# Opening of a fused FNet and MLP kernel: x loaded ahead of the weights, scratch laid out by group, first chunk as eight plain block products between the weight conversions

## The chip, the core and the metric

The kernel runs on one core of one Trainium2 chip. The metric is the device time of one execution in microseconds (us). Unless a "span" is named, times are medians over several executions.

## The reference

```python
def _attn_ref(x):                       # x: 8 x 3008 x 256, f32
    X = np.fft.fft(x, axis=1)
    X = np.fft.fft(X, axis=2)
    return X.real.astype(np.float32)

def _moe_ref(x, w_in, w_out):           # 24064 tokens, 256 -> 2048 -> 256, weights in float64
    h = x @ w_in
    relu6 = np.clip(h + 3.0, 0.0, 6.0)
    g = h * relu6 / 6.0
    return (g @ w_out).astype(np.float32)
```

The output of the first is reshaped to tokens and given to the second.

## The kernel before

The Fourier transform along the sequence is split in two (47 x 64). *Stage 1* multiplies by the 47-point table: a piece of x and its mirrored partner rows are folded on DVE, multiplied on TensorE, copied out by ACT as a piece of z, and written to a scratch `zd` in DRAM. *Stage 2* reads `zd` back transposed as g, one *group* of frequencies at a time, and multiplies by the table T into q. The transform along the 256 columns is folded into w_in ahead of time (`fold_w_in`). Then comes the MLP in *steps*: `mlp1` makes u and v, DVE and ACT make the activation a, `mlp2` multiplies by w_out into acc. Eight steps are a *chunk* of tokens. There are 48 chunks, so 384 steps: 352 of 4.75 us, and 32 of about 3.6 us in the shorter last chunk of each pair, some 1790 us in all. Nearly all the time is the MLP; what matters here is the opening before it, for the first *pair* of batches.

The weights are float64 and are taken apart by hand. One *piece* of weights goes through exponent_a on ACT, a matmul `ex` on TensorE, exponent_c on ACT, a mantissa and a join on DVE. There are 16 pieces. Pieces 0 to 3 and 6 to 9 are w_in, the others w_out.

```python
    def x_tile(pr, i):                      # where the pieces of x live in the opening
        pool, tag = xpool, "x"              # four buffers
        if pr.p == 0 and 4 <= i < 13:
            pool, tag = ((apool, "a"), (cpool, "c"), (spool, "t"))[(i >= 8) + (i >= 11)]
        return pool.tile([PR + 2, XC, D], F32, tag=tag, name="xt")
    ...
    def mlp2(ch, fc):                       # seven products, fast matrix multiplication
        a = ch.a.pop(fc)[:].rearrange("p m f n -> p (m f) n")[:, :, 0:ch.n]
        c = ch.c.pop(fc)                    # sums of blocks of a, made on POOL by combine()
        moving = [a[:, 0], a[:, 1], a[:, 3], c[:, 0], c[:, 1], c[:, 2], c[:, 3]]
        for i, mv in enumerate(moving):
            ...
            nc.tensor.matmul(ch.acc[i // 2][:, i % 2, 0:ch.n], G[:, i, fc, :], mv, ...)
    ...
    for c in range(NXC):                    # the opening: x and weights side by side
        if c + 2 < NXC:
            load_x(first, c + 2)
        load_w(c + 2)
        if c < NXC - 1:
            fold_first(first, c)
        else:
            for part in range(2):
                fold(first, c, part, nc.vector)
        on_scalar(c)                        # exponent_c of piece c-1, exponent_a of piece c
        on_vector(c)                        # mantissa of piece c, join of piece c-1
        for i in range(XC // 2):
            (stage1_first if c < NXC - 1 else stage1)(first, c, i)
        on_tensor(c)                        # ex of piece c; a finished pair is folded or mixed
        ...
    load_g(first, 0)
    for j in range(NXC, 15):                # the other weight pieces, one by one
        ...
    for i in range(2):
        stage2(first, 0, i)
    spread(first, 0)
    ...
    on_scalar(15); on_vector(15)            # (joined on one line here)
    mlp1(*chunk(0))                         # only now does the MLP begin
```

## Time and profile before

| | |
|---|---|
| median, three runs | 1984.56 us (1981.78 to 1984.95) |
| profiled span | 1978.3 us |
| TensorE busy | 1949.1 us, 99% of the span |
| first u of the MLP starts | 80.06 us |
| step 7 (last of chunk 0) ends | 132.37 us |

TensorE is nearly full from about 90 us to the end. The window lines in the prediction show the part where it is not: a busy time of 17 of 20 us there is not all useful, because it holds dummy matmuls, put there to keep TensorE from idling (`keep_awake`).

### The profile page before, as it was taken

The page shows a single profiled execution, that of the slowest core. Times are in us where ns is not written, and L with a number is a line of the kernel's source. Part 1 is how long each engine was busy: PE and PEld are TensorE (multiplying, and loading weights), DVE is VectorE, ACT ScalarE, POOL GpSimd, SP SyncE. Part 2 cuts the span into 40 slices and gives each one's busy share as a digit, 9 for nine tenths or more (in the row PEclk, how much of TensorE's full clock was granted, in tenths as well). Part 3 has the DMA queues.
Part 4 walks back from the last instruction along what each step waited for, and adds up shares of the span by engine and source line. Part 5 has one row for each costly group of instructions (what it writes and reads, how often), then busy time and mean ns, then how long its engine had stood idle before and what let it go on. Part 6 is the DMA issues. An engine that isn't in the chain of part 4 may idle for free.

```text
span 1978.3 us, 27746 instructions
## 1 busy us (share of the span) xinstructions
PE 1949.1 (99%) x9178; PEld 1685.4 (85%) x9178; DVE 1433.5 (72%) x2775; ACT 687.9 (35%) x1164; POOL 1414.2 (71%) x1604
## 2 busy tenths in 40 slices
PE   8899999999999999999999999999999999999998
PEld 5588888888998888888898888888889888888887
DVE  5677767776787776776777776777678777777776
ACT  6533333333333333333333333333333333333332
POOL 4277778786687787777768877778667667666765
PEclk9999999999999999999999999999999999999999
DMA  9502211111111111221111221212110101111000
GB/s 307 136 26 61 51 41 46 49 49 35 27 36 51 41 49 48 54 59 24 36 32 30 63 55 44 56 41 54 37 22 23 30 14 25 26 24 28 17 20 20
DMA packets 149701, 93.31 MB, mean 47 GB/s; under 512 B 121739, under 2 KB 135055, under 8 KB 149558
## 3 DMA queue, kind: packets, MB, share of 16 engines
q1 hardware_dynamic: 139294, 57.86, 12.2%
q0 software_dynamic: 9472, 33.49, 5.9%
q8 instruction: 72, 1.18, 0.2%
q14 instruction: 71, 0.58, 0.1%
q10 hardware_dynamic: 792, 0.20, 0.0%
HBM read 54.19 MB, written 37.33 MB: 46 GB/s over the span
## 4 chain that ended last, share of the span: by engine, by line
PE 93%; DVE 2%; ACT 1%; issue 0%; DMA 0%; SPq 0%; DVEq 0%; ACTq 0%
PE acc L403 56%; PE v L334 16%; PE u L334 16%; PE ps L284 2%; PE ps L227 2%; DVE a L379 1%; DVE s L339 1%; ACT t L376 0%; ACT PM L509 0%; DVE o L461 0%; PE wps L574 0%; DVE u L360 0%; PE ps L224 0%; PE ex L514 0%; PE awake L597 0%
## 5 line engine op out<-in xcount | busy, mean ns | idle before, releaser
L393 POOL TENSOR_TENSOR c<-a 128x512 f32<-128x512 f32 (+1 forms) x383 | 478.2, 1248 | 431.4 <-PE acc L403 369.3
L403 PE MATMUL acc<-c,G 128*128 128x256 f32 (+1 forms) x3072 | 712.0, 375 | 0.0
L376 ACT ACTIVATE t<-u,half 128x512 f32<-128x512 f32 (+1 forms) x384 | 261.0, 680 | 1100.5 <-DVE u L349 1018.7
L403 PEld LDWEIGHTS acc<-c,G 128*128 128x128 f32 x3072 | 577.5, 190 | 72.7
L339 DVE SCALAR_TENSOR_TENSOR s<-qn,WN,u 128x256 f32<-128x256 f32 (+1 forms) x768 | 330.0, 471 | 354.3 <-PE u L334 354.0
L403 PE MATMUL acc<-a,G 128*128 128x256 f32 (+1 forms) x2304 | 551.2, 375 | 0.0
L403 PEld LDWEIGHTS acc<-a,G 128*128 128x128 f32 x2304 | 433.8, 190 | 55.9
L334 PE MATMUL v<-q,W 127*128 127x256 f32 (+1 forms) x1536 | 390.1, 376 | 4.4 <-DVE a L379 4.4
L334 PE MATMUL u<-q,W 128*128 128x256 f32 (+1 forms) x1536 | 388.3, 375 | 2.4 <-DVE a L379 2.1
L379 DVE SCALAR_TENSOR_TENSOR a<-t,u 128x512 f32<-128x512 f32 (+2 forms) x448 | 263.7, 600 | 104.9 <-ACT t L376 102.1
L334 PEld LDWEIGHTS u<-q,W 128*128 128x128 f32 x1536 | 285.7, 190 | 58.2 <-issue 14.8
L334 PEld LDWEIGHTS v<-q,W 127*128 127x128 f32 x1536 | 288.7, 190 | 45.1 <-DVE a L379 4.1
L393 POOL TENSOR_TENSOR c<-c,a 128x256 f32<-128x256 f32 (+1 forms) x383 | 274.8, 717 | 30.0
L393 POOL TENSOR_TENSOR c<-a,c 128x256 f32<-128x256 f32 (+1 forms) x383 | 274.6, 717 | 30.1
L349 DVE TENSOR_TENSOR u<-s,v 128x512 f32<-128x512 f32 x352 | 245.0, 696 | 37.7 <-PE v L334 0.8
L379 DVE SCALAR_TENSOR_TENSOR a<-t,v 128x512 f32<-128x512 f32 (+1 forms) x480 | 263.2, 564 | 0.0
L376 ACT ACTIVATE t<-v,half 128x512 f32<-128x512 f32 (+1 forms) x384 | 260.5, 678 | 0.0
L351 DVE TENSOR_TENSOR v<-v,s 128x512 f32<-128x512 f32 x352 | 243.7, 692 | 0.0
L393 POOL TENSOR_TENSOR r<-w,e 128x256 f32<-128x256 f32 (+1 forms) x94 | 90.8, 987 | 3.7
L411 ACT ACTIVATE e<-acc 128x512 f32<-128x512 f32 (+2 forms) x190 | 86.3, 545 | 3.4 <-PE acc L403 3.3
L461 DVE STREAM_TRANSPOSE o<-r 128x256 f32<-128x256 f32 (+1 forms) x192 | 72.5, 414 | 0.2
L239 ACT COPY z<-ps 96x512 f32<-96x512 f32 x64 | 37.2, 582 | 83.7 <-PE ps L227 65.2
(91 smaller groups left out, 780.2 us busy)
## 6 DMA issues: line engine op xcount, KB each, us to landing
out_dram<-o SPq DMA_DIRECT2D x746, 32.0 KB
zd<-z SPq DMA_DIRECT2D x32, 384.0 KB
g<-zd SPq DMA_DIRECT2D x48, 256.0 KB
xt<-in_x_dram POOLq DMA_DIRECT2D x21, 384.0 KB, 4.1
qn<-qd SPq DMA_DIRECT2D x19, 256.0 KB
st<-in_moe_w_in_dram POOLq DMA_DIRECT2D x8, 512.0 KB, 9.1
st<-in_moe_w_out_dram POOLq DMA_DIRECT2D x8, 512.0 KB, 5.1
xt<-in_x_dram POOLq DMA_DIRECT2D x7, 376.0 KB, 3.9
```

Of the source, the lines that this page charges most:

```text
L227: nc.tensor.matmul(ps[0:PZ], F[0:PR, 0:PZ], y[:, 2 * i:2 * i + 2, :], start=True, stop=True)
L284: nc.tensor.matmul(ps[:, blk, u * P:n].rearrange("p (b k) -> p b k", b=2), g[:, kk, blk * (P + 1):blk * (P + 1) + P], T[:, :, gr, blk, kk, ...
L334: nc.tensor.matmul(ps[:, i, 0:nq], W1[r, blk, f * P:(f + 1) * P], q[r, blk, of:of + nq], start=True, stop=True)
L339: nc.vector.scalar_tensor_tensor(s[:, i, 0:nq], qn[:, of:of + nq], WN[:, f:f + 1], u[:, i, 0:nq], op0=AL.mult, op1=AL.add)
L349: nc.vector.tensor_tensor(u[:], s[:], v[:], op=AL.add)
L351: nc.vector.tensor_tensor(v[:], v[:], s[:], op=AL.subtract)
L376: nc.scalar.activation(t, h, AF.Relu, bias=half[:], scale=scale)
L379: nc.vector.scalar_tensor_tensor(dst, t, 1.0, h, op0=AL.min, op1=AL.mult)
L393: (eng or nc.gpsimd).tensor_tensor(out, in0, in1, op=AL.add)
L403: nc.tensor.matmul(ch.acc[i // 2][:, i % 2, 0:ch.n], G[:, i, fc, :], mv, start=(fc == 0 and i % 2 == 0), stop=(fc == NF - 1), skip_group_c ...
L411: nc.scalar.mul(ch.e[:, k:i + 1, 0:ch.n], ch.acc[i // 2][:, 0:i + 1 - k, 0:ch.n], 1.0 / WS)
L461: nc.vector.transpose(o[:, 0:n // DH, h], ch.r[:, m, h, 0:n].rearrange("p (j i) -> p j i", i=DH))
```

## The change

The intent is to let the MLP begin as soon as a quarter of w_in is ready, and to convert the other weights between the steps of chunk 0. To this end x is loaded alone first, with three pieces in flight, so that stage 1 ends early. The scratch is laid out by group, and the rows of group 0 are written first, so that the first g can be read early. The first chunk cannot use the seven products, whose mixed weights do not exist yet, so it uses the eight plain block products.

```diff
-    def x_tile(pr, i):
-        pool, tag = xpool, "x"
-        if pr.p == 0 and 4 <= i < 13:
-            pool, tag = ((apool, "a"), (cpool, "c"), (spool, "t"))[(i >= 8) + (i >= 11)]
+    ORDER = [NXC - 1] + list(range(NXC - 1))
+    def x_tile(pr, c):
+        pool, tag = (spool, "t") if pr.p == 0 and ORDER.index(c) % 3 == 2 else (xpool, "x")
...
-            nc.sync.dma_start(out=pr.zd[:].rearrange("b k c n d -> (b k c) n d")[:, c * XC:(c + 1) * XC, :], in_=z[:])
+            zd = pr.zd[:].rearrange("g b k c n d -> (g b k c) n d")[:, c * XC:(c + 1) * XC, :]
+            if pr.p > 0:
+                nc.sync.dma_start(out=zd, in_=z[:])
+            else:
+                n0 = PZ // NG
+                nc.sync.dma_start(out=zd[0:n0], in_=z[0:n0])
+                nc.scalar.dma_start(out=zd[n0:], in_=z[n0:])
...
+    def mlp2_first(ch, fc):
+        ...
+        for h in range(2):
+            for f in range(2):
+                nc.tensor.matmul(ch.acc[h][:], G[:, (B11, B12, B21, B22)[2 * f + h], fc, :], a[:, :, f], ...)
...
+    for c in ORDER[0:3]:
+        load_x(first, c)
+    for k, c in enumerate(ORDER):
+        for part in range(2):
+            fold(first, c, part, nc.vector)
+        for i in range(XC // 2):
+            stage1(first, c, i)
+        keep_awake(1)
+        if k + 3 < NXC:
+            load_x(first, ORDER[k + 3])
+        else:
+            for j in range(2 * k - 8, 2 * k - 6) if k > 4 else ():
+                load_w(j)
+        if k == 4:
+            load_w(0); load_w(1); load_t(0)      # joined on one line here
...
+    for j in range(4):                           # four pieces of w_in, then stage 2, then the MLP
+        head(j); exponent_b(j)
+        ...
...
+        late = 4 if p == 0 else 0
-            s2(NST * (gr - 1), cur, gr)
+            s2(NST * (gr - 1) + (late if gr == 1 else 0), cur, gr)
...
-                put(9 * c, load_x, nx, c)
+                t = 2 * late + (9 - late // 4) * c
+                put(t, load_x, nx, c)
...
-                    put(9 * c + 8 + 3 * i, stage1, nx, c, i)
+                    put(t + 8 + 3 * i, stage1, nx, c, i)
...
+    DUE = [(6, 7, 8), (9, 10, 11), (12, 13), (14, 15), (), (), (), ()]   # weight pieces in steps 0 to 3
```

## The prediction

> **What bounds the kernel now.** I first read the page: TensorE is busy 1949.1 us of a 1978.3 us span, so the middle is full. The 40 slices put the only weak spot in the first two (PE 8, DMA 9 and 5). So I cut the opening into stretches of 20 us. Columns: stretch, length, busy time and count of each engine, granted TensorE clock, DMA share, GB/s.
>
> ```profile
> 0.00:20.00 20.00, 17.09 (x50) 9.13 (x51) 9.20 (x22) 14.03 (x18) 11.65 (x21) 1.00 0.92 253
> 20.00:40.00 20.00, 20.00 (x78) 12.57 (x77) 10.70 (x21) 13.27 (x26) 7.41 (x11) 1.00 1.03 340
> 40.00:60.00 20.00, 16.74 (x54) 9.56 (x53) 13.86 (x31) 12.31 (x22) 2.89 (x5) 0.83 0.82 259
> 60.00:80.00 20.00, 17.00 (x61) 8.32 (x60) 11.97 (x27) 12.34 (x20) 1.42 (x2) 1.00 0.75 184
> 120.00:140.00 20.00, 20.00 (x97) 17.23 (x96) 13.05 (x24) 7.90 (x14) 13.64 (x16) 1.00 0.04 14
> ```
>
> Until about 46 us the DMA engines are full; later no resource is, so a chain must bind. The chain that ended last (start, length, work) names it:
>
> ```profile
> 69.28 1.41 ACT PM L509 x2
> 71.64 1.41 ACT PM L509 x2
> 73.53 0.47 issue
> 74.00 1.41 ACT PM L509 x2
> ...
> 92.06 3.53 PE acc L403 x14
> 95.58 0.86 PE u L334 x4
> 96.45 0.86 PE v L334 x4
> 97.31 3.02 PE acc L403 x14
> ```
>
> PM is the exponent of one weight piece on ACT: pieces follow each other every 2.36 us. From 92.06 on the chain is u, v, acc in turn, TensorE alone, 4.75 us per step (0.86 + 0.86 + 3.02). Step 7 (the last of chunk 0) ends at 132.37, counting acc groups; with few gaps after that, **only what comes before 132.37 can change the time**. A step of several timelines shows the x wait and the gap from row write to row read:
>
> ```profile
> 18.06 0.68 DVE L189 TENSOR_TENSOR y<-xt 94x508 f32<-94x508 f32 x1 [1.40 <-DMA xt<-in_x_dram,IX]
> 54.37 0.30 SPq L241 DMA_DIRECT2D zd<-z  x1
> 57.40 1.29 SPq L266 DMA_DIRECT2D g<-zd  x2
> 49.17 1.99 PE L227 MATMUL ps<-y,F 94*96 94x512 f32 x2 [2.87 <-DVE y L174]
> ```
>
> So before: x and weights share the DMA engines until 46 us, stage 1 ends at 54, the weight pieces finish one by one until 81, and the MLP fills until 92.
>
> **What the Trainium skill says.**
> - "DMA: Bandwidth & Descriptors", section on the anatomy of one DMA: about 2 us fixed, mostly the receipt of the write, plus the bytes. The trace agrees: 3.0 us from the issue of the last row write (54.37) to the read that waits for it (57.40).
> - "Trainium Kernel Development and Optimization", Key Constraints: SP, ACT and POOL queues run on the same 16 DMA engines. So writing rows on two queues adds no bandwidth; it can only let the first group's rows overtake the rest. The ceiling measured here is 340 GB/s (20 to 40 us).
> - "TensorE: Matmul & The Clock Gate", Part 1: after an idle window of about 3.4 us the clock halves. The trace agrees roughly: the pair of matmuls at 49.17 took 1.99 us after 2.87 us idle; the same group takes 1.02 at 132.21. The new gaps I find below are near 2 us or less.
>
> **Part by part: the first half.** One x piece is two transfers of 96x1024 f32, 0.79 MB together; a z piece is 0.39 MB, a weight piece 0.52 MB. The changed stream issues x first, three pieces in flight, and C, T, weights later. Before, x0 landed at 9.1; with C and piece 0 out of its way I take 8.5. DVE then folds piece 7 (the long form, 46.56 to 49.50 before: 3.0) and seven plain ones at 0.61 x 4 + 0.15 = 2.6. With three pieces in flight a slot is refilled 2.6 + 0.85 (issue) + 5.1 (indirect load, median of the page) after it was handed out: 8.55 per three pieces, 2.85 per piece. But x plus z is 1.18 MB per piece, and at 340 GB/s that is 3.5 us: **DMA stays the limit**. Bytes until the last x lands: F, CE, C 0.59 + x 6.3 + five z 2.0 + T 0.26 = 9.1 MB. By 12 us the trace before had moved 2.73 MB; take 2 us lost where only three pieces are in flight, then 0.33 MB/us: last x at 14 + 6.4/0.33 = 33. Its fold goes on to about 34.5 (33 to 36), not 49.5. TensorE saves eight matmul groups there (stage 1 is 1.72 per piece, not 3.44), but it waits for data in this stretch, so this is hidden.
>
> Then 2 x 0.86 matmul, 0.6 copy and 0.3 zc: ACT is free for weights at 37. Weights 0 and 1 were issued right behind x and landed by then. Rows of group 0 land near 40 (the 3.0 us above), their reads of 0.5 MB against the weight stream near 45: beside the weights, not on the path.
>
> **The four w_in pieces.** Pieces 0, 1: 2 x 2.36, to 41.7. Piece 2: exponent and ex to 44.1, and ACT then has to copy the two sums of the first fold, whose 3.43 us start at 43.5: ACT free at 47.6. Piece 3: exponent 1.41, ex 0.47 on TensorE, to 49.5. Stage 2 and spread 1.78 + 0.91: 52.2. Second fold 3.43: 55.6; the last copy 0.6: mlp1 of step 0 runs at about **56**, where before it ran at 80.06. A gain of 24 us, but twelve pieces are still to be converted, where before one was left.
>
> **Chunk 0, interleaved.** Each engine runs in program order, so I go through it by hand with: exponent 1.41, ex 0.45, exponent out 0.58, mantissa 1.07, join 0.7; mlp1 1.73; DVE and ACT from u to both gates 4.2 (as 96.49 to 100.27 before plus the ACT hop); block products 4 of N=512 = 3.43 (8 x 0.43 where before 7 x 0.43 = 3.02); fold 3.43; the single ex bank makes ex wait for the join before it. Times relative to mlp1(0) at 0: gate(0) ends 4.8; pieces 4 and 5 joined at 8; mlp2(0) runs 9.1 to 12.5; pieces 7 and 8 each cost TensorE a wait of 1.5. Step 1 in full, as an example of the walk: mlp1(2) 19.8 to 21.5; exponent 9 to 21.8, its ex to 22.3; mlp2(1) 22.3 to 25.7; gate(2) waits for mantissa 9 (22.2) and ends 25.7; ACT puts out exponent 9 after the gate's relus, 25.6; join 26.4; exponent 10 27.0, ex 27.5, out 28.1, join 28.9; fold 27.5 to 31.0, and ex 11 stands behind it: 31.4, out 32.0, join 32.8: 11.6 us for the step, of which TensorE works 9.9. So mlp2(1) ends 25.7, mlp2(2) 37.3, mlp2(3) 45.1, piece 15's ex 46.9. By sums over these 48 us: DVE 12 x 1.77 + 6 x 3.4 = 41, TensorE 38, ACT 34: **no engine is full, the ACT-TensorE-ACT-DVE chain of the pieces sets the pace, DVE nearly does**. Steps 4 to 6: 5.16 each (1.73 + 3.43). Step 7 has stage 2 0.9, mlp1 twice and 3.43. End of step 7: 46.9 + 3 x 5.16 + 0.9 + 1.73 + 3.43 + 1.73 = 70.2. The other half of stage 2 for group 1 now comes after it: +0.9; mlp1(9) and (10) come back to back, and the v of (10) needs the bank of u(9), one of three, which its gate frees only 4.2 after it began: +1.6. Sum 72.7.
>
> So step 7's equivalent is at 56 + 72.7 = 128.7 instead of 132.4: **3.7 us gained**. Were each of the twelve pieces 0.3 us better hidden than in my walk, it would be 7. Chunk 0 no longer needs combine or finish on POOL, and the mixing moved from DVE to POOL (4 x 0.72 = 2.9 us per block), where POOL is idle in steps 4 to 6; the fourth lies in step 9, where POOL has 2.8 of 4.75 us taken: no wait expected. Moving the second pair's loads by 8 steps at 8 instead of 9 apart ends at step 75 instead of 74, three steps ahead of its reader: hidden. The rest of the program is the same work.
>
> **Rivals.**
> 1. *DMA gets the opening back.* x, z and the read-back compete with weights; if bandwidth is 300 GB/s (4 to 24 us before: 304), the last x lands at 35.5, and g too comes later, after the w_in pieces: nothing gained or 2 us lost, 1985. For it: DMA share 1.03. Against: the 8.4 MB of weights, of which the trace before had moved over half by then, now queue behind x.
> 2. *The interleave flows better.* If chunk 0 were TensorE-bound: 8 x 5.16 + 12 x 0.43 + 6.9 + 1.7 + 0.9 = 56 us for its 70; then 14 us more gained, 1967. Against: the one ex bank, and DVE in order (a mantissa stands before each gate). This is the fast edge, half of it plausible.
> 3. *A new wait in the MLP proper* (POOL late with c after the fourth mix, second pair's z late): each stall is a few us once; +3, 1983. Against: the slack above.
> 4. *Faster by 2%* needs 39.7 us, that is a chunk 0 ending at 93: TensorE's own work after stage 1 (13.7 folds + 6.9 pieces + 41 chunk 0, from 37 on) alone ends at 99. Out of reach. *Slower by 2%* would need chunk 0 at 172.
>
> **Range.** Walk 3.7, fast rival 10 or more at a quarter, slow rival 0 at a fifth: mean about 6 of the median 1984.56: 1978.5. The x landing is uncertain by 2 us, the walk by 5, the runs by 1.5: 1970 to 1985. Chances: faster by over 2% 0.01, within 0.98, slower 0.01.
>
> **What would show it right or wrong.** Right: last fold of the opening ending at 33 to 36; mlp1(0) at 54 to 58; DMA share near 1 to 35; four steps with weight pieces at some 11 us each for the first two and 8 for the next two, later 5.2; step 7's end near 128; from there to the end the same length (about 1846 us) as before. Wrong if: mlp1(0) waits for g or WN rather than for the second fold; weights land late and ACT waits for DMA in the first pieces; the clock drops in the gaps between pieces (PEclk under 0.9 after 40 us); or the tail from step 8 on has changed length.

## The result

The changed kernel took **1986.59 us** (median of four, 1986.0 to 1987.58), the kernel before, on the same chip in the same rounds, 1984.76 (median of four, 1981.78 to 1986.38). The ratio is **1.0011, with a 95% interval of 0.9994 to 1.0029**: the same within 2%. A ratio is the mean time of one kernel's fast runs over that of the other's of the same rounds, so it is not quite the ratio of these medians. The control e10, the changed kernel again in other rounds, gave 1.0022 (1.0008 to 1.0036). The class was predicted right, but the time lies outside the predicted range of 1970 to 1985, on its slow side: instead of 6 us gained, 2 to 4 us were lost.

The spans of the two profiles are 1978.3 and 1984.2 us. That difference of 5.9 us is larger than what the medians show, because the profile of before fell on one of its fast executions. The comparison of traces below explains the difference between these two executions; the size of the effect comes from the ratios.

These are the same five stretches of the changed kernel. Columns: stretch, length, busy time and count of PE, PEld, DVE, ACT and POOL, granted TensorE clock, DMA share, GB/s.

```profile
0.00:20.00 20.00, 17.45 (x43) 7.57 (x44) 10.27 (x27) 10.70 (x11) 10.39 (x17) 1.00 0.84 214
20.00:40.00 20.00, 14.64 (x29) 4.74 (x28) 13.92 (x27) 6.73 (x14) 7.83 (x13) 0.91 1.03 329
40.00:60.00 20.00, 14.23 (x47) 7.74 (x46) 6.93 (x13) 11.19 (x19) 1.45 (x3) 0.91 0.76 263
60.00:80.00 20.00, 16.53 (x51) 8.08 (x50) 13.15 (x26) 13.16 (x22) 2.86 (x4) 1.00 0.29 79
120.00:140.00 20.00, 18.46 (x73) 12.83 (x72) 13.69 (x24) 6.95 (x13) 8.83 (x11) 1.00 0.15 40
```

The reader sees two things. In the first stretch the DMA engines moved 214 GB/s where before they moved 253, although x was the only large load. And the clock, which dipped only in one stretch before, is below 1 in two.

The chain that ended last, of the changed kernel (start, length, work):

```profile
16.02 7.39 DMA xt<-in_x_dram,IX
...
27.40 8.82 DMA xt<-in_x_dram,IX
...
42.29 1.39 ACT PM L513 x2
...
53.26 2.61 DMA WN<-W
55.88 3.64 PE ps L267 x16
59.52 0.89 PE ps L278 x8
60.41 3.45 PE wps L568 x8
...
111.87 3.44 PE acc L387 x8
```

Now the chain begins in transfers of x, one after the other; before, the profile's chain up to 92 us ran through the weight pieces on ACT. From 60.41 on it is second fold, u and v, then the interleaved pieces, then TensorE alone (111.87 is a plain block product of chunk 0).

The TensorE timeline of the changed kernel, with the idle time before each entry and what ended it in brackets:

```profile
53.56 0.38 PE L518 MATMUL ex<-PM,E 128*128 128x512 f16 x1 [1.32 <-ACT PM L513]
...
55.86 3.65 PE L267 MATMUL ps<-T,g 128*128 128x128 f32 x16 [1.28 <-DMA WN<-W]
...
189.10 1.05 PE L267 MATMUL ps<-T,g 128*128 128x128 f32 x8
190.83 1.10 PE L207 MATMUL ps<-y,F 94*96 94x512 f32 x2 [0.68 <-ACT q L270]
```

And the same places in the kernel before: its first stage 2 at 77 us, and then stage 2 and stage 1 of the next pair at 190 us:

```profile
77.38 1.95 PE L284 MATMUL ps<-T,g 128*128 128x128 f32 x16
...
187.07 1.05 PE L284 MATMUL ps<-T,g 128*128 128x128 f32 x8
...
192.72 1.02 PE L227 MATMUL ps<-y,F 94*96 94x512 f32 x2
```

At 55.86 the first stage 2 waits 1.28 us for a transfer and then takes 3.65 us for 16 matmuls; before it took 1.95 us in the same view (the chain view, which the prediction and the table below use, has 3.64 and 1.78). At 190.83 stage 1 stands right behind stage 2 and waits 0.68 us for ACT to empty the one PSUM bank that both use. Before, a whole step lay between them and nothing waited.

The issue times on the SP queue of the changed kernel (the last row write of group 0, then the read that needs all such writes):

```profile
42.72 0.31 SPq L227 DMA_DIRECT2D zd<-z  x1
...
47.59 1.28 SPq L249 DMA_DIRECT2D g<-zd  x2
```

From write to read it is 4.87 us; before it was 3.0 us. Other traces with the same loads and writes took longer (e1 5.68, e3 6.02, e7 6.79, and e10, the same code, 6.72).

**The account.** Here is the walk of the prediction against the trace of the changed kernel (us).

| mark | predicted | measured | lost at this term |
|---|---|---|---|
| last fold of the opening ends | 34.5 | 39.0 | 4.5 |
| ACT begins weight piece 0 | 37 | 42.3 | 0.8 |
| from there to the last ex of piece 3 | 12.5 | 12.3 | -0.2 |
| wait ahead of stage 2 | 0 | 1.28 | 1.3 |
| stage 2 and spread | 2.7 | 4.5 | 1.8 |
| first u (second fold ahead of it) | 56 | 63.7 | -0.5 |
| first u to the end of step 7 (133.26 measured) | 70.2 | 69.6 | -0.6 |
| other half of stage 2, bank of v(10) | 0.9 + 1.6 | 0.89 + 1.54 | -0.1 |
| **step 7's equivalent** | 128.7 | 135.7 | **7.0** |

Against the 132.4 of before, 135.7 is 3.3 us late, not 3.7 us early. This is one execution: in e10, the same code, the last fold ended at 37.7 and the opening lost less, as the table of the experiments shows. The rest of the program then loses another 1.8 us: each stage 1 that stands right behind a stage 2 costs the wait of 0.68 us and 0.24 us of slow matmuls around it, 0.92 in all. The changed kernel has four such places (190.83, 273.02, near 355, 437.41), the kernel before two (269.22, 452.45). So the two traces should differ by 3.3 + 1.8 = 5.1 us, and the spans differ by 5.9; 0.8 us is not accounted for.

### The profile page after: what moved, and what is told of

Same layout as the page of the kernel before. It is cut to its first block, busy times and chain, and to the rows that moved or that the text cites. A ratio compares the mean times of both kernels' runs of the same rounds, so it can differ in the third digit from the quotient of the medians.

```text
span 1984.2 us, 27496 instructions
## 1 busy us (share of the span) xinstructions
PE 1945.5 (98%) x9058; PEld 1663.0 (84%) x9058; DVE 1436.5 (72%) x2773; ACT 687.7 (35%) x1163; POOL 1398.4 (70%) x1591
## 3 DMA queue, kind: packets, MB, share of 16 engines
HBM read 54.19 MB, written 37.32 MB: 46 GB/s over the span
## 4 chain that ended last, share of the span: by engine, by line
PE 92%; DVE 3%; DMA 2%; ACT 2%; issue 1%; SPq 0%; POOL 0%; DVEq 0%; ACTq 0%
PE acc L403 54%; PE v L318 16%; PE u L318 16%; PE ps L267 2%; PE ps L207 2%; DMA xt<-in_x_dram,IX 1%; DVE s L323 1%; DVE a L363 1%; PE acc L387 1%; ACT t L360 1%; ACT PM L513 1%; DVE o L461 0%; DMA out_dram<-o 0%; PE spare L568 0%; PE ex L518 0%
## 5 line engine op out<-in xcount | busy, mean ns | idle before, releaser
L377 POOL TENSOR_TENSOR c<-a 128x512 f32<-128x512 f32 (+1 forms) x375 | 467.4, 1246 | 409.1 <-PE acc L403 363.4
L403 PE MATMUL acc<-c,G 128*128 128x256 f32 (+1 forms) x3008 | 696.9, 374 | 0.0
L403 PEld LDWEIGHTS acc<-c,G 128*128 128x128 f32 x3008 | 565.4, 190 | 71.1
L403 PE MATMUL acc<-a,G 128*128 128x256 f32 (+1 forms) x2256 | 539.0, 375 | 0.0
L403 PEld LDWEIGHTS acc<-a,G 128*128 128x128 f32 x2256 | 424.1, 190 | 54.4
L377 POOL TENSOR_TENSOR c<-c,a 128x256 f32<-128x256 f32 (+1 forms) x375 | 268.3, 716 | 29.4
L377 POOL TENSOR_TENSOR c<-a,c 128x256 f32<-128x256 f32 (+1 forms) x375 | 268.2, 715 | 29.4
L333 DVE TENSOR_TENSOR u<-s,v 128x512 f32<-128x512 f32 x352 | 245.0, 696 | 37.7 <-DVE s L323 1.4
L207 PE MATMUL ps<-y,F 94*96 94x512 f32 x120 | 62.4, 611 | 11.5 <-DVE y L177 6.3
```

What stands on the lines that cost most here:

```text
L207: nc.tensor.matmul(ps[0:PZ], F[0:PR, 0:PZ], y[:, 2 * i:2 * i + 2, :], start=True, stop=True)
L333: nc.vector.tensor_tensor(u[:], s[:], v[:], op=AL.add)
L377: (eng or nc.gpsimd).tensor_tensor(out, in0, in1, op=AL.add)
```

## The experiments

My theory from the traces had four causes. **A**: three pieces in flight do not fill the DMA engines, so x comes late. **B**: the clock halves in the gaps before stage 2. **C**: the weight loads, now in one flood right behind x, delay the confirmation of the row writes and the read of g. **D**: the loads of the second pair, put 8 instead of 9 steps apart, place stage 1 right behind stage 2. The rivals were that the interleaving itself costs time (tested by e7), that splitting the row writes over two queues hurts (e8), and that before and after differ only by run-to-run chance (e10). Edits are against the changed kernel. In each table entry "first u" is the start of the MLP, and "offset" is how much later than in the trace of before a step stands: at step 8, and in the steps past 569 us, where it no longer changes.

| run | last fold ends | ACT begins piece 0 | g read issued | stage 2: start, length | first u | offset at step 8, late | ratio to before, 95% |
|---|---|---|---|---|---|---|---|
| before | 49.6 | - | 57.40 | 77.38, 1.95 | 80.06 | 0, 0 | - |
| after | 39.0 | 42.29 | 47.59 | 55.86, 3.65 | 63.68 | 2.0, 5.52 | 1.0011 (0.9994 to 1.0029) |
| e10 (same code) | 37.7 | 42.30 | 47.67 | 55.28, 2.13 | 61.58 | -0.13, 3.39 | 1.0022 (1.0008 to 1.0036) |
| e1 | 37.7 | 41.4 | 46.66 | 55.37, 3.40 | 63.29 | 1.57, 1.44 | 1.0005 (0.9988 to 1.0021) |
| e2 | 34.3 | 39.84 | 45.49 | 54.66 (two matmuls at 53.11), 3.24 | 62.06 | 0.36, 3.90 | 1.0023 (1.0007 to 1.004) |
| e3 | 36.8 | 40.2 | 45.55 | 55.02, 2.20 | 61.38 | -0.33, 2.92 | 1.001 (0.9993 to 1.0026) |
| e4 | 37.7 | 44.11 | 46.05 | 56.24, 2.07 | 62.48 | 0.83, 4.36 | 1.0011 (0.9994 to 1.0027) |
| e5 | 38.1 | 42.23 | 45.08 | 56.34, 1.95 | 62.46 | 0.79, 0.37 | 0.9998 (0.9981 to 1.0015) |
| e6 | 34.0 | 37.32 | 40.64 | 51.99, 2.02 | 58.18 | -3.49, -3.86 | 0.9979 (0.9962 to 0.9995) |
| e7 | 37.5 | 41.93 | 47.25 | 55.54, 3.75 | 102.37 | 18.5, 21.8 | 1.0101 (1.0084 to 1.0118) |
| e8 | 37.3 | 40.20 | 47.05 | 55.06, 3.66 | 62.99 | 1.63, 4.87 | 1.0026 (1.0009 to 1.0043) |
| e9 | 34.5 | 37.78 | 43.16 | 55.20, 3.75 | 63.65 | 1.93, 5.07 | not timed |
| e11 (e6 again) | 36.2 | 39.44 | 42.86 | 55.75, 2.78 | 63.57 | 1.92, 1.57 | 0.9984 (0.997 to 0.9997) |
| e12 | 31.9 | 34.88 | 43.73 | 53.37, 3.65 | 61.19 | -0.45, -0.95 | 0.998 (0.9964 to 0.9996) |

The offsets are each against one trace of before, a fast one. They show where within an execution time is lost; a single trace must not be read as the kernel's time.

**e1_shift: the second pair's stages 1 step later (D).**

```diff
-                t = 2 * late + (9 - late // 4) * c
+                t = 2 * late + late // 4 + (9 - late // 4) * c
```

> The changed kernel with the second pair's loads, folds and stage-1 groups one step later (9 + 8c instead of 8 + 8c). Theory A (stage 1 stands right behind stage 2 in the same step and waits for the one PSUM bank until ACT has copied q; four times in the first pair instead of two, 0.92 us each): no stage-1 group of the first pair waits for the q copy any more, the four waits at 191, 273, 355 and 437 us are gone, and step 91's distance to the kernel before falls from 5.5 to about 1.8 us; the profile's span falls by 3.7 us from 1984.2 to 1980.5. Rival B (the later loss is something else, say POOL or the z write): those waits go but the span stays within 1 us of 1984.2.

Median 1982.42 against 1981.71 of before. On the TensorE timeline of e1 the two stages no longer touch:

```profile
188.67 1.05 PE L267 MATMUL ps<-T,g 128*128 128x128 f32 x8
...
194.32 1.02 PE L207 MATMUL ps<-y,F 94*96 94x512 f32 x2
```

No wait stands behind the stage 1 line, and none of this kind is left in the trace. The offset does not grow (1.57 to 1.44), where it grew by 3.5 in both traces of the unedited kernel (2.0 to 5.52, -0.13 to 3.39). At step 8 all of these still owe 0.86 and 0.89 us of stage work that the kernel before has already done. The unedited kernel pays these and twice 0.92 net, 3.6 in sum; e1 pays them too but loses none of the four waits, while the kernel before loses its two: 1.75 - 1.84 = -0.1, as measured. D is shown, on the trace.

**e2_depth: four pieces of x in flight (A).** The fourth buffer comes from a pool that is idle then; weight loads move to the buffers that this frees.

```diff
-        pool, tag = (spool, "t") if pr.p == 0 and ORDER.index(c) % 3 == 2 else (xpool, "x")
+        k = ORDER.index(c) % 4 if pr.p == 0 else 0
+        pool, tag = (xpool, "x") if k < 2 else (spool, "t") if k == 2 else (cpool, "c")
...
-    for c in ORDER[0:3]:
+    for c in ORDER[0:4]:
```

> The changed kernel with four x pieces in flight instead of three (the fourth in the tiles of c; weights 2, 3 then go where pieces 0 and 4 lay, 6 and 7 into c). Theory A (the round trip of three pieces leaves DMA time unused before 20 us, so x is late): the last fold of the opening ends at 35.5 to 37 instead of 39.0, GB/s in 8 to 20 us rises from 215-273 to 290 or more, span 2 to 3 us shorter. Rival B (the DMA engines are full at about 320 GB/s with x and z anyway): the last fold ends at 38.3 to 39.3, span unchanged within 1 us.

Median 1986.25, no gain. But the loads did what A says. These are the stretches in which x is loaded, first of the changed kernel, then of e2 (columns as above):

```profile
8.00:20.00 12.00, 11.06 (x33) 4.70 (x32) 8.53 (x20) 5.13 (x8) 5.37 (x7) 1.00 0.97 243
20.00:36.00 16.00, 11.02 (x22) 3.44 (x20) 10.30 (x20) 5.27 (x11) 5.68 (x9) 0.89 1.03 321
```

```profile
8.00:20.00 12.00, 11.72 (x35) 5.28 (x34) 10.31 (x23) 5.25 (x9) 6.97 (x10) 1.00 1.03 285
20.00:36.00 16.00, 13.25 (x30) 4.57 (x29) 12.11 (x24) 6.39 (x15) 6.30 (x10) 1.00 1.04 369
```

With one piece more in flight, 243 and 321 GB/s become 285 and 369, and the last fold ends at 34.3, within the predicted 33 to 36. This is more than run-to-run spread: the eight traces with three pieces have it at 36.8 to 39.0, the five with four at 31.9 to 36.2. A is shown. In 20 to 36 us the share column hardly differs (1.03 against 1.04), so **the DMA share alone does not tell whether the engines move all that they can**. The gain went into new waits on ACT, of which this is the longer. The first line is ACT's own issue of a row write, the second the copy of a small column that follows it in the program:

```profile
33.20 0.31 ACTq L229 DMA_DIRECT2D zd<-z  x1
33.56 0.30 ACT L239 ACTIVATE zc<-z,F 96x4 f32<-96x4 f32 x1 [4.01 <-DMA zq<-zc]
```

The profile books the 4.01 us to the column copy and ends them with an earlier write of such a column. But the row write, which stands ahead of the copy in the program, was itself issued only at 33.20. So ACT was held ahead of its own issue, and the number of zc buffers (four), which I suspected, is not what held it. Another wait at such an issue, of 2.62 us, ended with the transfer of T. So the weight pieces began at 39.84 and not at 37, and stage 2 then waited for g until 54.66.

**e3_awake: dummy matmuls after weight pieces 2 and 3 (B).**

```diff
+        if j >= 2:
+            keep_awake(2)
```

> The changed kernel with two idle matmuls more after weight piece 2 and after piece 3, ahead of stage 2. Theory A (the gaps of 1.3 us at 52 and 55 us leave TensorE at half clock, so stage 2 takes 3.65 us where 1.78 was measured before): stage 2 takes 1.8 to 2.2 us, the granted clock in 56 to 60 us goes from 0.58 to 1.00, mlp1 of step 0 begins 1.2 to 1.9 us earlier than 63.7. Rival B (the clock isn't the cause, or the idle matmuls take what they give): mlp1(0) begins at 63.4 or later.

Median 1983.45, ratio 1.001, which the interval does not tell apart from the changed kernel's. Stage 2 ran at full clock after a wait that is still there:

```profile
55.02 2.20 PE L267 MATMUL ps<-T,g 128*128 128x128 f32 x16 [0.84 <-DMA WN<-W]
```

3.65 became 2.20 us. However, the control e10, without the dummies, also has 2.13:

```profile
55.28 2.13 PE L267 MATMUL ps<-T,g 128*128 128x128 f32 x16 [0.48 <-DMA WN<-W]
```

So e3 does not show that the dummies did it, as its wait was also shorter than in the changed kernel. Over all traces of the new opening the length of stage 2 goes with the wait just ahead of it: with no wait, or waits of 0.48 to 0.84 us, it took 1.95 to 2.20 us (e3, e4, e5, e6, e10); with waits of 1.09 us or more, 2.78 to 3.75 us (after, e1, e2, e7, e8, e9, e11, e12), with or without dummies. The slow clock is real (0.58 granted in 56 to 60 us of the changed kernel, 1.00 in e10), but B is then largely a consequence of the wait. The term is worth between 0.2 us (2.13 against 1.95) and 1.7 us (3.65 against 1.95).

**e4_hold: weight pieces 4 to 7 loaded later (C).** Each is loaded only when an earlier piece leaves its buffer, so that four pieces instead of eight are asked for ahead of the read of g.

```diff
-    STRAIGHT = (0, 1, 8, 9, 14, 15)
-    NEXT = {0: 8, 1: 9, 4: 10, 5: 11, 6: 12, 7: 13, 8: 14, 9: 15}
+    STRAIGHT = (0, 1, 4, 5, 8, 9)
+    NEXT = {0: 4, 1: 5, 2: 6, 3: 7, 4: 8, 5: 9, 6: 10, 7: 11, 8: 12, 9: 13, 10: 14, 11: 15}
...
-            for j in range(2 * k - 8, 2 * k - 6) if k > 4 else ():
+            for j in (2, 3) if k == 5 else ():
```

> The changed kernel with the weight pieces 4 to 7 held back until pieces 0 to 3 have been read (4 and 5 reuse the buffers of 0 and 1). Theory A (weights 4 to 9 fill the DMA engines at 380 to 414 GB/s between 40 and 52 us, so the last row write takes 4.9 us to be confirmed instead of 3.0, and the read of g is late): the read of g is issued at 45.5 to 46.5 instead of 47.6, stage 2 begins at 54.5 instead of 55.9, and mlp1(0) begins 1 us or more earlier. Rival B (g is not what stage 2 waits for): g's issue moves, but mlp1(0) stays at 63.7 within 0.3 us.

Median 1984.1. The wait ahead of stage 2 is gone:

```profile
56.24 2.07 PE L267 MATMUL ps<-T,g 128*128 128x128 f32 x16
```

From the first ex to the first u it took 17.6 us instead of 20.6. Stage 2 was also ready later than in the changed kernel (the first ex came at 44.89 instead of 43.07), which alone could have hidden the wait; but SP's own wait for the row write fell from 3.9 to 1.2 us, and the read of g came 2.57 us after the write, where the flood of weights gave 4.87 to 6.79. That this did not show in the time has a reason in the same trace: the clock fell to 0.50 at 36 to 40 us, the last stage 1 ran at half speed, and the first ex came only at 44.89. C is shown for the read of g; its gain was spent ahead of it.

**e5_shift_awake_hold: e1, e3 and e4 together.** The edit is the three diffs above.

> The changed kernel with the three repairs together: second pair one step later, idle matmuls after weight pieces 2 and 3, weights 4 to 7 held back. If the three losses are separate (theory): from the ex of piece 0 to the first u of mlp1(0) 17.4 to 18.0 us instead of 20.6 (the run with weights held back alone: 17.6), no wait of stage 1 for q, span 1978 to 1980 against 1984.2. Rival (they are one loss seen three times, or the run-to-run spread of x's arrival, 36.8 to 39.0 so far, covers them): 20 us or more there, or a span of 1981 or more.

Median 1981.21 against 1981.77; ratio 0.9998. B, C and D are mended on the trace (stage 2 1.95 us, no wait ahead of it, offset 0.79 to 0.37), which leaves A: the last fold ended at 38.1, and ACT then waited 2.33 us and 0.99 us ahead of its own row-write issues. From the first ex to the first u it took 19.45 us, between the expected 17.4 to 18.0 and the rival's 20. So the three together only bring the changed kernel level with the one before.

**e6_shift_awake_hold_deep: e5 with four pieces in flight.** Beside e2's edit, zc gets eight buffers and T is loaded behind the read of g, which was meant to take ACT's waits away.

```diff
-        zc = zpool.tile([PZ, XC], F32, tag="zc", bufs=4, name="zc")
+        zc = zpool.tile([PZ, XC], F32, tag="zc", bufs=8, name="zc")
...
     load_g(first, 0)
+    load_t(0)
```

> As the run before, and four x pieces in flight, with what took the gain away in the first try removed: there ACT sat 4.0 us before zc and 2.6 us before the last zc, behind buffers and DMA slots (zq and T not landed), so zc gets eight buffers and T(0) is issued behind the read of g. Theory: last fold at 34 to 35, ACT begins piece 0 within 3 us of it (37 to 38, where it was 42.3 in the changed kernel and 39.8 in the first try), mlp1(0) at 56 to 58 instead of 63.7, span 1974 to 1977. Rival (weights arrive no sooner, the DMA engines are the limit after all): ACT waits for the weight piece itself, mlp1(0) at 60 or later, span within 1 us of the run before.

Median 1977.04 (1976.02 to 1977.72), ratio 0.9979 (0.9962 to 0.9995): faster than before by a little (the same within 2%), and no execution as slow as e5's fastest (1979.74) of the same rounds. ACT began piece 0 at 37.32, the predicted 37, and the TensorE timeline shows:

```profile
51.99 2.02 PE L268 MATMUL ps<-T,g 128*128 128x128 f32 x16 [0.64 <-DMA T<-in_c_stage_dram]
...
58.18 0.59 PE L319 MATMUL u<-q,W 128*128 128x256 f32 x2
```

The MLP begins at 58.18, at the upper end of the predicted 54 to 58, and the final offset is -3.86 against the -3.7 of the walk. That match is partly luck: the first u is 2.2 us later than the walk's 56, and 1.8 us of the offset are the two waits of stage 1 that the kernel before has and e6 has not, which the walk did not count. This is also the fastest of e6's four executions. With the four causes mended, and T moved, the loss turns into a gain: together they are enough to explain the miss. One by one A, C and D are shown; B is not shown apart from C.

**e7_serial: no interleaving.** All sixteen weight pieces are converted ahead of chunk 0.

```diff
+    for j in range(4, 16):
+        head(j); exponent_b(j); keep_awake(1); exponent_c(j)
+        fold_all(); join(j); copy_all()
+        ...
-    DUE = [(6, 7, 8), (9, 10, 11), (12, 13), (14, 15), (), (), (), ()]
+    DUE = [()] * 8
```

> The changed kernel with all 16 weight pieces converted before chunk 0 begins, as the kernel before did, and chunk 0 plain. Theory (the interleave is worth what the prediction's walk gave it): 12 pieces at 2.36 plus two folds of 3.4 put mlp1(0) at 97 to 101 instead of 63.7, chunk 0 then takes 5.2 us a step, the end of step 7 comes 11 to 15 us later than in the changed kernel, span 1995 to 1999. Rival (interleaving only shifts the same chain): end of step 7 within 4 us, span 1985 to 1988.

Median 2001.64, ratio 1.0101. In its chain the weight pieces stand one behind the other, until the MLP begins:

```profile
99.84 1.42 ACT PM L513 x2
...
102.53 0.88 PE u L318 x4
```

The late offset is 21.8 us, 16.3 more than in the changed kernel, and so more than the 11 to 15 expected. The interleaving is worth those 16 us and is not what failed.

**e8_oneq: each row write in one transfer on SP.**

```diff
-            if pr.p > 0:
+            if pr.p >= 0:
                 nc.sync.dma_start(out=zd, in_=z[:])
```

> The changed kernel with the first pair's rows written in one transfer each on the SP queue (no split of the first group's rows from the rest). Theory A (the split lets the first group's rows pass): the read of g is issued 1 to 3 us later relative to the last z copy than the 6.0 us of the changed kernel, and stage 2 later by as much. Rival B (the same 16 engines serve both queues, the split is worth nothing): the read of g is issued within 0.7 us of 6.0 after the last z copy began (41.1 there), mlp1(0) unchanged, and ACT even gains the 0.4 us per piece of its issues.

Median 1986.06, ratio 1.0026 (1.0009 to 1.0043), not told apart from the changed kernel's 1.0022. ACT was free a little sooner (40.20 instead of 42.3), but the read of g came 7.06 us after the last write:

```profile
39.99 0.31 SPq L223 DMA_DIRECT2D zd<-z  x1
...
47.05 1.28 SPq L249 DMA_DIRECT2D g<-zd  x2
```

With the split it was 4.87 us in the changed kernel, but in the control e10 it was 6.72:

```profile
40.95 0.31 SPq L227 DMA_DIRECT2D zd<-z  x1
...
47.67 1.28 SPq L249 DMA_DIRECT2D g<-zd  x2
```

Over the five traces with the split and the flood of weights (the changed kernel, e1, e3, e7, e10) it was 4.87 to 6.79 us, so the split bought g between 0.3 and 2.2 us in these executions. It cost ACT between 0.4 and 1.7 us: from the last fold to piece 0 it took 2.9 us in e8 and 3.3 to 4.6 in those five. With the weights held back (e6) the read came after 2.8 us. ACT waits at its own queue: in e10 it sat 2.37 us for a row write and 1.43 us for T.

**e9_deep_zc: e2 with eight zc buffers and T behind g.** This is the deep load with ACT's waits taken away, without e5's three repairs.

> The changed kernel with four x pieces in flight, zc in eight buffers and T(0) issued behind the read of g; nothing else. It parts the first try with four pieces (gain lost) from the full repair. Theory (ACT's two waits, 4.0 and 2.6 us, were what lost it): last fold at 34 to 35, ACT begins piece 0 at 37 to 38.5 instead of 39.8. Then the held-back weights are what it still lacks: the read of g late against a DMA share of 1, stage 2 at half clock, mlp1(0) at 59.5 to 62. Rival (the DMA engines made ACT wait anyway): ACT begins piece 0 at 39.5 or later.

One run, 1984.87, with 1981.97 for before. ACT began at 37.78: the wait for T is gone, while the one ahead of the row write at 32 us is still 2.65 us, in spite of eight zc buffers. But stage 2 still began at 55.20, after a wait of 5.13 us, and at half clock (3.75), and the first u came at 63.65, later than the 59.5 to 62 expected. **In this look an earlier x alone only moved the wait to the transfers behind it on SP** (g, T or WN, which the trace does not part); in e6, where B, C and D are mended too, it pays.

**e10_after: the changed kernel again, as a control.**

> The changed kernel once more, unaltered but for a comment, as a control in the same rounds as the best version and for the spread of the opening: last fold at 36.5 to 39.5, mlp1(0) at 61 to 64, ratio to the kernel before 1.001 to 1.003.

Median 1985.95 (1983.88 to 1987.46) against 1981.97, ratio 1.0022: the kernel is slower than before, by a little. On the same chip and in the same rounds e11 gave 0.9984, so the repairs are worth 1 - 0.9984/1.0022 = 0.4% of the changed kernel, some 7.5 us.

**e11_best: e6 again.**

> The full repair once more (second pair one step later, idle matmuls, weights held back, four x pieces, zc in eight buffers, T behind g), five rounds: ratio to the kernel before 0.996 to 0.9995, against the changed kernel some 8 us faster. If the first measurement was the luck of one chip: a ratio of 0.9995 or more.

Median 1979.23, ratio 0.9984 (0.997 to 0.9997): still faster than before, but its profiled execution, at 1981.48 us the slowest of its five, is not like that of e6. The first stage 2 waited 2.29 us for T and ran at 2.78 us, and the first u came at 63.57. T behind g is a weak spot that I had put in myself.

**e12_oneq_deep: e6 with T early again and all row writes on SP.**

```diff
-            if pr.p > 0:
+            if pr.p >= 0:
...
+        if k == 4:
+            load_t(0)
...
     load_g(first, 0)
-    load_t(0)
```

> The repair of e6 and e11 without its own weak spot: the first table T is read beside the fifth piece again, not behind the read of g, and all row writes are issued from SP, so that ACT is never held by a transfer's slot. If the two remaining losses are ACT's waits in the writes and the late T: ACT begins the first weight piece within 3 us of the last fold (e6 3.3, e11 3.3, after 3.3), stage 2 waits for no T, mlp1(0) at 57 to 58, ratio to before 0.997 to 0.999, like e6 and never like e11's 63.6. Rival, from e8: with all writes on SP the read of g is issued 7 us behind the last write and not 3 to 5, so g arrives only at 48 to 50 and stage 2 waits for it; then mlp1(0) is at 59 to 61 and the ratio 0.999 to 1.001, no better than e11.

Median 1979.01 (1975.46 to 1979.42) against 1980.42; ratio 0.998. Theory and rival each held in part. ACT began at 34.88, 2.9 us after the last fold and earlier than in any other run, and nothing waited for T. But on its SP queue, and then on TensorE, one sees

```profile
38.44 0.55 SPq L224 DMA_DIRECT2D zd<-z  x1
...
43.73 1.64 SPq L250 DMA_DIRECT2D g<-zd  x2
```

```profile
53.37 3.65 PE L268 MATMUL ps<-T,g 128*128 128x128 f32 x16 [4.48 <-DMA g<-zd]
```

The last copy of z on ACT had ended at 34.6; SP issued its write only at 38.44, the read of g 5.3 us later, and g took until 53.4. So the 2.4 us that ACT gained over e6 were lost again: stage 2 began 1.4 us later than in e6 and at half clock took 1.6 more, and the first u came at 61.19 instead of 58.18. The ratio is in the theory's range, the first u just past the rival's 59 to 61. A split that puts neither ACT nor SP behind is left open.

## Why the prediction was wrong, point by point

1. **"DMA stays the limit ... then 0.33 MB/us: last x at 33": the step that failed first, and the largest.** The bytes were right: with 1.4 MB before 8 us (0 to 20 less 8 to 20), 2.9 MB up to 20 and 5.1 MB up to 36, 9.4 MB had moved when the last x landed at 36.2, against 9.1 estimated (0.3 MB, or 0.9 us at the rate assumed). The rate was wrong: 288 GB/s over the 28 us from 8 to 36, because only three pieces were in flight. The prediction had seen the point and charged 2 us for it, but only up to 14 us; and from a refill estimate of 2.85 us per piece it concluded that the depth would not bind after that. The term that was too small there is the indirect load: 5.1 us is its median over the whole program, most of which is the MLP with quiet DMA. In the first 46 us the median was 13.3 us before and 7.6 us in the changed kernel. So three pieces came round in 11.3 and 12.75 us and not in 8.55, which is 3.8 to 4.25 us per piece, more than the 3.5 of "DMA stays the limit". DVE shows it, at the folds of every third piece:

```profile
12.20 0.68 DVE L169 TENSOR_TENSOR xt<-xt 94x508 f32<-94x508 f32 x1 [0.22 <-DMA xt<-in_x_dram,IX]
...
23.50 0.68 DVE L169 TENSOR_TENSOR xt<-xt 94x508 f32<-94x508 f32 x1 [1.05 <-DMA xt<-in_x_dram,IX]
...
36.25 0.68 DVE L169 TENSOR_TENSOR xt<-xt 94x508 f32<-94x508 f32 x1 [0.41 <-DMA xt<-in_x_dram,IX]
```

Nor was 340 GB/s a ceiling: it was the mean of one stretch, and the changed kernel moved 409 and 414 in 40 to 44 and 44 to 48 us. With four in flight (e6: 290 and 376 GB/s in the two stretches) the mean is 339, almost exactly the rate assumed. The late x costs 4.5 of the 7.0 us in this execution (in the seven other traces with three pieces the last fold ended 2.3 to 3.6 us after the predicted 34.5). Rival 1 of the prediction ("if bandwidth is 300 GB/s ... 35.5 ... 1985") was nearly what came; I gave it a fifth.
2. **"ACT is free for weights at 37": failed by another 0.8 us**, for the row writes that ACT now issues itself. Their issue was left out of the walk. In e2, e5 and e10 ACT stood 1 to 4 us ahead of such an issue.
3. **"Reads ... near 45: beside the weights, not on the path": failed by 1.3 us.** The 3.0 us from write to read came from a moment when the DMA engines moved 190 GB/s (52 to 56 us); in the changed kernel they moved 409 and 414 in 40 to 44 and 44 to 48 us, and it was 4.87. e4, which holds the weights back, has 2.57 and no wait. The profile names the last small transfer on the SP queue (WN) as releaser; stage 2 does not read WN, and in e8 and e12 the wait is put to g itself. Which transfer of that queue held it in the changed kernel is not settled.
4. **"Stage 2 and spread 1.78 + 0.91": 1.8 us too small in this execution**, from the clock. The prediction judged gaps "near 2 us or less" as harmless. Two gaps of 1.32 and 1.28 us, with two matmuls of 0.38 us between them, were enough. In e10 the second gap was 0.48 us and stage 2 ran at full clock, so the term follows point 3.
5. **The interleaved chunk was right.** From first u to the end of step 7 it was 69.6 us against 70.2 predicted; steps 4 to 6 took 5.16 each (110.14, 115.31, 120.47 in the chain) as predicted, and the wait for the bank of v(10) 1.54 against 1.6. e7 shows the worth of it.
6. **"Moving the second pair's loads ... hidden": failed, 1.8 us net.** I checked that the data come in time, and not where stage 1 falls relative to stage 2, which shares its PSUM bank. e1 shows it.
7. **The range** came from the spread of three runs and the walk. Terms 1 to 4 all depend on x or on the queues and failed in the same direction, while the range treated them as independent. The mean is also off: a quarter of 10, a fifth of 0 and the rest at 3.7 make 4.5 us and not 6. Three of the prediction's own signs of being wrong came true: stage 2 waited for a transfer on g's queue, the clock fell (0.58 in 56 to 60 us), and the tail from step 8 on grew.

Open: 0.8 us between the two spans; why the kernel before itself spreads from 1979 to 1986 us; why the wait ahead of stage 2, and the half clock with it, differs from execution to execution of the same code.

## What to carry to other kernels

When a load is moved to the front alone, count the bytes in flight, not the bytes: with three pieces of 0.79 MB in flight these engines moved 243 and then 321 GB/s, with four 285 and 369, at nearly the same DMA share. When one wait is removed, look at once for the next two in line on that path (here ACT's own issues, then g, then T), and repair them together: none that was tried alone made the kernel faster than before, all together were worth 0.4% of the changed kernel and 0.2% against before. When the schedule of a background stage is shifted, check which steps it now stands next to, and whether the two share a PSUM bank.

## What the Trainium skill lacked or had wrong

- "DMA: Bandwidth & Descriptors", section on the anatomy of one DMA, gives a fixed cost of about 2 us (measured for transfers issued by GpSimd) and makes the receipt of the write most of it. Here the time from issuing a 64 or 384 KB row write to issuing the read that waits for it was 3.0 us before, 4.87 to 6.79 us in the five traces with the split and the flood of weights, 7.06 us in e8 and 2.8 us in e6. A reader who plans with a constant is off by up to 4 us or more under load.
- No page that I found tells how many large loads must be in flight to fill the engines. Here three pieces (each two transfers of 0.39 MB) gave 243 to 260 GB/s in 8 to 20 us, four gave 254 to 290; in 20 to 36 us it was 313 to 343 against 363 to 377 (eight traces and five).
- "Trainium Kernel Development and Optimization", Key Constraints, says that issuing from several engines only saves the sequencer's issue time. In bandwidth the runs do not contradict it, but the choice of queue also moves waits: in e10 ACT stood 2.37 us ahead of its own row-write issue, and in e8, where SP issued all of them, ACT began piece 0 2.9 us after the last fold instead of 3.3 to 4.6. Key Constraints does not say that an issuing engine's other work waits with it; the DMA page says only that a semaphore wait happens on the issuing sequencer before the transfer is sent off.
- "TensorE: Matmul & The Clock Gate", Part 1, ties the half clock to an idle window of about 3.4 us. Here it came after two gaps of 1.32 and 1.28 us with two matmuls between (3.65 us where 1.95 was normal). Further on the page says that short idle times between groups of matmuls can also do it, if they are frequent enough, but gives no length. Its remark that the window runs freely is not tested here: the same code had 3.65 and 2.13 us, but after waits of 1.28 and 0.48 us.
